# Order of transfer issues in the first chunk, and a weight load cut into ten alternating pieces, in an mLSTM and feed-forward kernel

## The chip, the cores and the metric

The kernel runs on one core of one Trainium2 chip. The time is the device time of one execution in microseconds; it is given as the median of several runs. A core has five engines that run side by side, each through its own list of instructions in order: TensorE (PE, with its weight loads as PEld), VectorE (DVE), ScalarE (ACT), GpSimd (POOL) and SyncE (SP), which here issues nearly all DMA transfers. They meet through semaphores: an instruction that waits holds everything behind it on its engine. The transfers themselves are done by 16 DMA engines. Data that is computed on lies in SBUF (128 partitions), the results of matmuls in PSUM.

## The reference

```python
for t in range(S):                                   # mLSTM, per batch and head, S = 768, D = 40
    m_new  = max(f[t] + m, i[t])
    f_stab, i_stab = exp(f[t] + m - m_new), exp(i[t] - m_new);  m = m_new
    C = f_stab * C + i_stab * outer(v[t], k[t])      # C is 40 x 40
    n = f_stab * n + i_stab * k[t]
    y[t] = sigmoid(o[t]) * (C @ q[t]) / max(abs(n . q[t]), 1)
x = y as (4 * 768) tokens x (8 heads * 40)           # 3072 x 320
h = x @ w_in                                         # 320 x 2048
out = max(0.01 * h, h) @ w_out                       # 2048 x 320
```

There are 4 batches and 8 heads. All arrays are float32 but for the two weight matrices, which come as 8-byte floats: the kernel reads them as 64-bit words and narrows them to float32 itself.

## The kernel before, in words

**Chunks and steps.** The sequence is cut into NB = 6 chunks of 128 positions. A step s is one chunk of one batch: s = 4c + b, steps 0 to 23. The recurrence becomes, per chunk, a 128 x 128 matrix of decays and scores per head, plus a state C carried from chunk to chunk. The feed-forward part of chunk c - 1 is woven into the cell work of chunk c, in units whose order is written out by hand: PE, DVE, ACT and POOL run in the order of the program (`manual_schedule`, L742). SP is not in that list; the framework's scheduler places its transfers.

**The cell part.** `gates(c)` (L237) makes the running sums and maxima of the gates of a chunk for all 32 batch-heads on VectorE, two exponentials on ScalarE, stores the results a and exp(a) to a small DRAM buffer `a_dr` (L254, L260), and for c = 2 and 3 loads the gates of chunk c + 2 (`load_fi`, L262). `u_gates(c)` (L643) transposes its results on PE and copies them to gT and gL on VectorE. `feed(s)` (L665) loads k and v of a step (L302) and spreads a from `a_dr` over the 128 partitions (`spread`, L334). `load_blocks(s, i)` (L312) loads k, q or o_gate of a step in 32-partition blocks, four transfers of 80 KB each (L320). `spread_q` (L336) spreads exp(a) over two halves of 64 partitions (L342). `ahead(s)` (L652) prepares step s: the exponentials of the decays on ScalarE (L376), transposes of k and q on VectorE (L414, L420), then the block loads and `spread_q` of step s + 2, the gated v on GpSimd, and the mask of step s + 1 on GpSimd (`prep_mask`, L368). `u_scores(s)` and `u_mix(s)` are the matmuls of a step; `u_mix` ends by storing x to DRAM (L545), from where `gather_x` (L548) brings it back transposed.

**Buffers.** k/q and v have 4 buffers (step modulo 4), the blocks `rb` and `ea` 2, the decays `w` 4, the gates `fi` 2, the raw weights `raw` 2.

**The weights.** Each matrix is loaded in four quarters: n = 0 to 3 are w_in, n = QN = 4 to 7 are w_out; the text calls them w(0) to w(3), and QN to QN+3. `load_weights(n)` (L171) issues the transfers, `narrow_weights(n)` (L202) is one ScalarE instruction (L213) and six on VectorE (L215 to L229). w_in is laid out in two halves of 64 partitions r = 0, 1, each with five slots of 256 columns; a half takes the five 64-row slices of the matrix in the order `SLOTS[r]`, which is (0, 2, 4, 1, 3) or (1, 3, 0, 2, 4). A quarter of w_in is loaded in four transfers: in each half one that takes three slices with a step of two (384 KB) and one of two slices (256 KB); the first half is issued whole ahead of the second. A quarter of w_out is one transfer of 1280 KB over 128 partitions.

**The first chunk** (`first_chunk`, L669) does steps 0 to 3 with a path of its own: `load` takes k, q and v at once, the scores need PE transposes, `u_x` (L562) brings x to the feed-forward layout by PE and five ScalarE copies. It also narrows w(0) and w(1) and does the first two feed-forward units. Then L744 to L756 issue what chunk 1 needs.

**Chunk 1** (the loop at L764 with c = 1) has 30 units i of the feed-forward part of chunk 0: units 0 to 13 are halves of the first matmul (L588), 14 to 29 are parts of the second (L623), one for each block of tokens and quarter of w_out. `todo` says at which unit a weight quarter is narrowed, `fetch` at which one a quarter of w_out is loaded, `place` after which ones a cell unit follows: scores of step 4 at i = 2, mix of step 4 at 7, scores of 5 at 9, mix of 5 at 11, and so on. After each `u_mix(s)` come the o_gate blocks of s + 2 and `feed(s + 4)`.

Of the kernel before, what the change touches and what calls it, by code (L numbers as in the profile page):

```python
# [18 lines left out]
def kernel(  # L19
# [26 lines left out]
    nc = tc.nc  # L46
    B, H, S, D = q.shape
    P = 128
# [40 lines left out]
    def load_fi(c):  # L89
        t = fi[c] = wk.tile([BH, 2, P], F32, name="fi")  # L90
        eng = nc.scalar if c < 3 else nc.sync
        eng.dma_start(t[:, 0, :], f_all[:, ts(c, P)])
        eng.dma_start(t[:, 1, :], i_all[:, ts(c, P)])
# [69 lines left out]
    def run_of(r, at):  # L163

        ks = SLOTS[r][at:]
        return ks[0], next((i for i in range(1, len(ks)) if ks[i] != ks[i - 1] + 2), len(ks))
# [4 lines left out]
    def load_weights(n):  # L171

        if n < QN:
            dst = w_in[:, n, :]
        else:
            dst = w_out[:, 4 * (n - QN) : 4 * (n - QN + 1), :].rearrange("p a d -> p (a d)")
        to = dst
        if wide:
            if n < 2:
                at = NF * GT - 2 * WC * (n + 1)  # L180
                raw = acts_l[:, at : at + 2 * WC].bitcast(U64)
            elif n == QN:
                raw = w_out[:].rearrange("p f d -> p (f d)")[:, 2 * WC : 4 * WC].bitcast(U64)
            else:
                raw = wk.tile([P, dst.shape[1]], U64, name="raw")[:]
            raws[n] = (raw, dst)
            to = raw
        if n < QN:
            for r in range(2):
                cols = slice(n * QC + 2 * P * r, n * QC + 2 * P * (r + 1))  # L190
                src = moe_w_in[:, cols].rearrange("(k p) c -> p k c", p=DP)
                half = to[DP * r : DP * (r + 1), :].rearrange("p (k c) -> p k c", k=KC)
                at = 0
                while at < KC:
                    k0, n_k = run_of(r, at)
                    nc.sync.dma_start(half[:, at : at + n_k, :], src[:, k0 : k0 + 2 * n_k - 1 : 2, :])
                    at += n_k
        else:
            rows = moe_w_out[(n - QN) * QC : (n - QN + 1) * QC, :]
            nc.sync.dma_start(to.rearrange("p (a d) -> p a d", d=Dm), rows.rearrange("(a p) d -> p a d", p=P))  # L200
# [90 lines left out]
    def load(s):  # L291
        c, b = divmod(s, B)
        rows = ts(c, P)
        d = st[s] = {"kq": kq_t[s % NL], "va": va_t[s % NL]}
        if c == 0:
            parts = [(d["kq"][:, 0, :, :D], k), (d["kq"][:, 1, :, :D], q), (d["va"][:, :, :D], v)]
        else:
            parts = [(d["kq"][:, 0, :, :D], k)] + [
                (d["va"][:, :, QW * n : QW * n + DB], v[:, :, :, DB * n : DB * (n + 1)]) for n in range(2)
            ]  # L300
        for dst, src in parts:
            nc.sync.dma_start(dst, src[b, :, rows, :].rearrange("h p d -> p h d"))  # L302
# [9 lines left out]
    def load_blocks(s, i):  # L312

        c, b = divmod(s, B)
        src = (k, q, o_gate)[i][b, :, ts(c, P), :]
        for r in range(2):
            for n in range(2):
                at = QW - n * (DB if i == 2 else QW)
                rows = slice((2 * r + n) * QW, (2 * r + n + 1) * QW)
                nc.sync.dma_start(  # L320
                    rb_t[s % NR][rows, i, at : at + RL].rearrange("p (j w) -> p j w", j=PR),
                    src[r::2].rearrange("j (p n) d -> p j (n d)", n=TB),
                )
# [12 lines left out]
    def spread_q(s):  # L336

        c, b = divmod(s, B)
        d = st[s]
        d["ea"] = wk.tile([P, PR, P], F32, name="ea", bufs=EAB)  # L340
        for r in range(2):
            nc.sync.dma_start(  # L342
                d["ea"][DP * r : DP * (r + 1)], a_dr[c, 1, b * H + r : (b + 1) * H : 2, :].partition_broadcast(DP),
            )
# [320 lines left out]
    def feed(s):  # L665
        load(s)
        spread(s)

    def first_chunk():  # L669

        for n in range(B):
            load(n)
        load_o(0)
        load_o(1)
        load_weights(0)
        load_o(2)
        load_o(3)
        for n in range(1, 3):
            load_weights(n)
        bu, a = gates(0)  # L680
        warm(14)
        gates_T(0, bu)
        u_transpose(0)
        spread_first(a, 0)
        prep_exp(0)
        prep_vu(0)
        prep_vu(1)
        prepare_tiles()
        u_transpose(1)
        u_scores(0)  # L690
        u_state(0)
        prep_exp(1)
        spread_first(a, 2)
        bus[1] = gates(1)
        u_scores(1)
        u_values(0)
        u_state(1)
        u_transpose(2)
        prep_o(0)
        gate(0)  # L700
        prep_exp(2)
        prep_vu(2)
        w = narrow_weights(0)
        next(w, None)
        u_values(1)
        u_scores(2)
        prep_o(1)
        gate(1)
        u_state(2)
        for _ in w:  # L710
            pass
        u_transpose(3)
        prep_exp(3)
        prep_vu(3)
        prepare_step(0)
        prepare_step(1)
        u_x(0)
        u_values(2)
        u_scores(3)
        u_x(1)  # L720
        u_state(3)
        prep_o(2)
        gate(2)
        w = narrow_weights(1)
        for _ in range(4):
            next(w, None)
        ffs = ff_units(0)
        ffs[0]()
        u_values(3)
        prep_o(3)  # L730
        gate(3)
        u_x(2)
        ffs[1]()
        for _ in w:
            pass
        u_x(3)
        prepare_step(2)
        prepare_step(3)
        return ffs

    E = mybir.EngineType
    with tc.manual_schedule(engines={E.PE, E.DVE, E.Activation, E.Pool}):  # L742
        ffs = first_chunk()
        feed(B)  # L744
        spread_q(B)
        for i in range(3):
            load_blocks(B, i)
        load_weights(3)
        feed(B + 1)
        spread_q(B + 1)  # L750
        for i in range(3):
            load_blocks(B + 1, i)
        load_weights(QN)
        feed(B + 2)
        feed(B + 3)
        load_fi(3)  # L756


        ffs = ffs[2:]
        todo = {0: 2, 3: 3, 8: QN, 12: QN + 1, 17: QN + 2, 22: QN + 3}  # L760
        fetch = {4: QN + 1, 7: QN + 2, 16: QN + 3}
        place = (2, 7, 9, 11, 13, 15, 17, 18, 19)
        now = iter(())
        for c in range(1, NB + 1):  # L764
            if c > 1:
                ffs = ff_units(c - 1)
            cells = cell_units(c) if c < NB else []
            n_ff, n_c = len(ffs), len(cells)
            lead = 2 if c == 1 else 0
            done = fed = 0  # L770
            waiting = []
            for i in range(n_ff):
                if c == 1:
                    if i in todo:
                        for _ in now:
                            pass
                        now = narrow_weights(todo[i])
                    next(now, None)
                    next(now, None)
                    if i in fetch:  # L780
                        load_weights(fetch[i])
                    if i == 0:
                        prep_mask(B)
                        u_gates(1)
                        ahead(B)
                if i == lead and c + 1 < NB:
                    bus[c + 1] = gates(c + 1)
                ffs[i]()
                upto = sum(p <= i for p in place) if c == 1 else min(n_c, (i + 1) * n_c // (n_ff - 8))
                while done < upto:  # L790
                    fn, s = cells[done]
                    fn(s)
                    done += 1
                    if fn is u_scores:
                        ahead(s + 1)
                    elif fn is u_mix:
                        waiting.append(s)
                if i >= n_ff // 2 - 1:
                    for s in waiting:
                        gather_x(s)  # L800
                    waiting.clear()
                while fed < done:
                    fn, s = cells[fed]
                    fed += 1
                    if fn is u_mix:
                        if s + NR < NS:
                            load_blocks(s + NR, 2)
                        if s + NL < NS:
                            feed(s + NL)
# [31 lines left out]
```

## Time and profile before

| | |
|---|---|
| median of 11 runs | 584.75 us (582.55 to 587.31) |
| the profiled execution | 584.8 us, its span 583.0 us |
| mean granted clock of TensorE | 0.941 |
| PE busy | 545.2 us, 94% of the span |
| DVE, ACT, POOL busy | 256.6, 154.5, 110.2 us |
| moved by DMA | 69.89 MB, 120 GB/s in the mean |
| DMA packets | 158412, of these 87072 under 512 B |
| chain that ended last | PE 77%, DVE 10%, DMA 7%, SP's queue 2% |

The profile divides the span into 40 slices and gives each engine's busy share in tenths. Other views list the instructions of an engine in order of time (start, duration, engine, line, operation, and in brackets the idle time before it with what ended it), sum up who waited for whom, follow back the chain of work that ended last, or give sums for chosen windows: the window, its length, then the busy time of PE, PEld, DVE, ACT and POOL with the number of instructions, the granted clock, the share of time that the 16 DMA engines were busy, and the rate in GB/s. "SPq" is SP's own queue: the issuing of a transfer, not the transfer. An issue that takes long stands behind a queue that takes no more.

### The profile page before, as it was taken

How to read it: one execution, taken by the hardware profiler on the slowest of the kernel's cores; microseconds unless marked ns; L12 is line 12 of the kernel's file. 1: busy time of each engine (PE TensorE's matmuls, PEld its weight loads, DVE VectorE, ACT ScalarE, POOL GpSimd, SP SyncE). 2: the span in 40 equal slices, each digit the busy share in tenths (PEclk: the TensorE clock that was granted, in tenths of full speed). 3: DMA queues.
4: the chain of work that ended last, by engine and by line, in shares of the span. 5: the costliest groups of instructions: out<-in, count | busy, mean ns of one | idle time of the engine just before them, and what ended most of it. 6: DMA issues, size and time to landing. Idle time of an engine off the chain costs nothing.

```text
span 583.0 us, 9166 instructions
## 1 busy us (share of the span) xinstructions
PE 545.2 (94%) x3456; PEld 362.6 (62%) x3456; DVE 256.6 (44%) x423; ACT 154.5 (26%) x401; POOL 110.2 (19%) x128
## 2 busy tenths in 40 slices
PE   8988799786569999999999999999999999999997
PEld 7976788554345556765556765566754567744575
DVE  4589779997142643523552704562305552000000
ACT  4465433410004331104341004331023320022100
POOL 4145223153100333110333301331202000000000
PEclk9569779897869999999999999999999999999999
DMA  9998995974851754752665643755533021100000
GB/s 119 168 196 194 176 227 147 271 162 123 214 136 38 162 144 134 176 127 59 156 149 135 160 118 78 164 141 129 162 89 90 26 63 57 45 12 0 1 22 22
DMA packets 158412, 69.89 MB, mean 120 GB/s; under 512 B 87072, under 2 KB 151200, under 8 KB 158368
## 3 DMA queue, kind: packets, MB, share of 16 engines
q1 hardware_dynamic: 157984, 69.18, 50.9%
q8 instruction: 27, 0.44, 0.3%
q10 hardware_dynamic: 384, 0.13, 0.1%
q14 instruction: 17, 0.14, 0.1%
HBM read 61.90 MB, written 7.37 MB: 119 GB/s over the span
## 4 chain that ended last, share of the span: by engine, by line
PE 77%; DVE 10%; DMA 7%; SPq 2%; issue 1%; POOL 1%; ACT 1%; ACTq 0%; DVEq 0%; POOLq 0%
PE ph L588 32%; PE po L623 32%; PE sc L443 3%; PE pT L519 3%; PE pT L525 3%; DMA a_dr<-a 2%; DMA raw<-in_moe_w_out_dram 2%; PE dC L455 2%; DVE kqT L414 1%; DVE kq L420 1%; PE pa L493 1%; DVE w_out L229 1%; DMA va<-in_v_dram 1%; DMA w<-a_dr 1%; DVE w L447 1%
## 5 line engine op out<-in xcount | busy, mean ns | idle before, releaser
L623 PE MATMUL po<-w_out,acts 128*128 128x320 f32 x768 | 221.1, 448 | 20.8 <-DVE w_out L229 17.6
L588 PE MATMUL ph<-xT,w_in 64*128 64x512 f32 (+1 forms) x1120 | 221.3, 546 | 6.4 <-ACT acts L596 6.4
L623 PEld LDWEIGHTS po<-w_out,acts 128*128 128x128 f32 x768 | 148.4, 196 | 86.7 <-DVE w_out L229 18.7
L588 PEld LDWEIGHTS ph<-xT,w_in 64*128 64x128 f32 x1120 | 113.2, 195 | 96.6 <-issue 86.4
L596 ACT ACTIVATE acts<-ph 128x512 f32<-128x512 f32 (+1 forms) x112 | 53.5, 532 | 147.7 <-PE ph L588 147.6
L447 DVE TENSOR_TENSOR w<-w,sc 128x512 f32<-128x512 f32 x48 | 30.8, 681 | 125.2 <-PE sc L443 125.2
L376 ACT ACTIVATE w<-w,gT 128x128 f32<-128x128 f32 x192 | 58.7, 394 | 19.2 <-DVE gL L287 16.2
L628 ACT COPY y<-po 128x320 f32<-128x320 f32 x24 | 10.2, 425 | 195.5 <-PE po L623 185.6
L368 POOL TENSOR_TENSOR w<-w,cmask 128x1024 f32<-128x1024 f32 x20 | 48.0, 2400 | 48.0 <-DMA w<-a_dr 38.2
L466 POOL TENSOR_TENSOR C<-C,gL 64x168 f32<-64x168 f32 x32 | 17.4, 545 | 189.5 <-PE pT L519 188.3
L414 DVE STREAM_TRANSPOSE kqT<-rb 128x512 f32<-128x512 f32 x40 | 41.1, 1103 | 2.7 <-DMA rb<-in_k_dram 2.7
L531 DVE STREAM_TRANSPOSE hb<-pT 128x512 f32<-128x512 f32 x20 | 14.3, 715 | 57.7 <-PE pT L525 57.7
L525 PE MATMUL pT<-w,va 128*64 128x128 f32 x320 | 32.4, 276 | 1.8 <-ACT rb L403 1.5
L538 POOL TENSOR_TENSOR xb<-xb,den 128x320 f32<-128x320 f32 x20 | 14.5, 727 | 100.9 <-DVE xb L535 97.3
L519 PE MATMUL pT<-kq,C 128*64 128x128 f32 x320 | 32.7, 280 | 0.0
L443 PEld LDWEIGHTS sc<-kqT 40*128 40x128 f32 x384 | 27.4, 205 | 8.5 <-issue 8.0
L420 DVE TENSOR_TENSOR kq<-kqT,ea 40x512 f32<-40x512 f32 x40 | 29.0, 725 | 1.4
L443 PE MATMUL sc<-kqT 40*128 40x128 f32 x384 | 29.1, 294 | 0.0
L542 DVE STREAM_TRANSPOSE x<-xb 128x512 f32<-128x512 f32 x20 | 22.2, 1111 | 8.3 <-POOL xb L538 8.3
L525 PEld LDWEIGHTS pT<-w,va 128*64 128x64 f32 x320 | 21.5, 139 | 2.2 <-ACT rb L403 1.7
L519 PEld LDWEIGHTS pT<-kq,C 128*64 128x64 f32 x320 | 20.1, 138 | 2.4 <-issue 2.4
L455 PEld LDWEIGHTS dC<-vu,kq 128*64 128x64 f32 x320 | 12.3, 151 | 13.7 <-issue 10.4
(94 smaller groups left out, 277.9 us busy)
## 6 DMA issues: line engine op xcount, KB each, us to landing
w<-a_dr SPq DMA_DIRECT2D x20, 512.0 KB
rb<-in_k_dram SPq DMA_DIRECT2D x80, 80.0 KB
rb<-in_q_dram SPq DMA_DIRECT2D x80, 80.0 KB
rb<-in_o_gate_dram SPq DMA_DIRECT2D x80, 80.0 KB
ea<-a_dr SPq DMA_DIRECT2D x40, 128.0 KB
kq<-in_k_dram SPq DMA_DIRECT2D x24, 160.0 KB
raw<-in_moe_w_out_dram SPq DMA_DIRECT2D x3, 1280.0 KB
xT<-x_dr SPq DMA_DIRECT2D x40, 96.0 KB
```

The source lines that it names most:

```text
L368: nc.gpsimd.tensor_tensor(w[:], w[:], cmask[:].unsqueeze(1).to_broadcast([P, H, P]), op=ALU.add)
L376: nc.scalar.activation(w[:, h, :], w[:, h, :], AF.Exp, bias=gT[c][:, 0, bh : bh + 1], scale=1.0)
L414: nc.vector.transpose(in_blocks(d["kqT"][:, i]), raw_blocks(s, i, QW).rearrange("p (j n) d -> p j n d", n=TB),)
L420: nc.vector.tensor_tensor(d["qs"][rows], d["kqT"][rows, 1], d["ea"][rows].rearrange("p j t -> p (j t)"), op=ALU.mult,)
L443: nc.tensor.matmul(sc[r][:, j, :], lhsT=kqT[rows, 0, ts(j, P)], rhs=kqT[rows, 1, ts(j, P)], start=True, stop=True,)
L447: nc.vector.tensor_tensor(w[:, r::2, :], w[:, r::2, :], sc[r][:], op=ALU.mult)
L455: nc.tensor.matmul(dC[rows, h // 2].rearrange("p k d -> p (k d)"), lhsT=d["kq"][:, 0, h, :], rhs=d["vu"][:, h].rearrange("p k d -> p (k d) ...
L519: nc.tensor.matmul(pT[DP * r : DP * (r + 1), ts(j, P)], lhsT=C[:, b, j, r, :], rhs=d["qs"][:, ts(j, P)], start=True, stop=False,)
L525: nc.tensor.matmul(pT[DP * r : DP * (r + 1), ts(j, P)], lhsT=d["va"][:, h], rhs=d["w"][:, h, :], start=False, stop=True,)
L588: nc.tensor.matmul(ph[r][:, cols], lhsT=w_row(r, slot, j), rhs=xT[DP * r : DP * (r + 1), slot, cols], start=(slot == 0), stop=(slot == KC ...
L596: nc.scalar.activation(acts[:, f, cols], ph[r][:, cols], AF.Prelu, alpha=0.01)
L623: nc.tensor.matmul(po[n][:], lhsT=acts[:, f, ts(n, P)], rhs=w_out[:, f, :], start=(f == 0), stop=(f == NF - 1),)
```

## The change

1. A quarter of w_in is loaded in ten transfers, one for each slot and half (64 partitions x 256 columns, 128 KB), and the two halves alternate.
2. `load_blocks` issues its four transfers in the order of partitions 0, 64, 32, 96, where it was 0, 32, 64, 96.
3. `u_gates(1)` moves from unit 0 of chunk 1 into the first chunk, between `u_values(1)` and `u_scores(2)`.
4. `gates(2)`, with its two stores and the loads of the gates of chunk 4, moves from unit 2 of chunk 1 into the first chunk, ahead of `u_x(3)`.
5. `feed(6)` and `feed(7)` move from ahead of chunk 1 to its units 2 and 6, so behind the block loads of steps 6 and, for `feed(7)`, of step 7. `load_fi(3)` moves to unit 0, behind `ahead(4)`.
6. The loads of QN+1 and QN+2 move from units 4 and 7 to 5 and 8; QN+2 so comes behind what follows the mix of step 4.

`st.setdefault` only lets `spread_q` come ahead of `load` for a step.

```diff
-            for r in range(2):
-                cols = slice(n * QC + 2 * P * r, n * QC + 2 * P * (r + 1))
-                src = moe_w_in[:, cols].rearrange("(k p) c -> p k c", p=DP)
-                half = to[DP * r : DP * (r + 1), :].rearrange("p (k c) -> p k c", k=KC)
-                at = 0
-                while at < KC:
-                    k0, n_k = run_of(r, at)
-                    nc.sync.dma_start(half[:, at : at + n_k, :], src[:, k0 : k0 + 2 * n_k - 1 : 2, :])
-                    at += n_k
+            src = moe_w_in[:, n * QC : (n + 1) * QC].rearrange("(k p) (r c) -> r p k c", p=DP, r=2)
+            for slot in range(KC):
+                for r in range(2):
+                    nc.sync.dma_start(
+                        to[DP * r : DP * (r + 1), 2 * P * slot : 2 * P * (slot + 1)], src[r, :, SLOTS[r][slot], :],
+                    )
...
-        for r in range(2):
-            for n in range(2):
+        for n in range(2):
+            for r in range(2):
...
         u_values(1)
+        u_gates(1)
         u_scores(2)
...
         for _ in w:
             pass
+        bus[2] = gates(2)
         u_x(3)
...
         load_weights(QN)
-        feed(B + 2)
-        feed(B + 3)
-        load_fi(3)
...
-        fetch = {4: QN + 1, 7: QN + 2, 16: QN + 3}
+        fetch = {5: QN + 1, 8: QN + 2, 16: QN + 3}
...
-            lead = 2 if c == 1 else 0
...
                     if i == 0:
                         prep_mask(B)
-                        u_gates(1)
                         ahead(B)
-                if i == lead and c + 1 < NB:
+                        load_fi(3)
+                    if i in (2, 6):
+                        feed(B + 2 + i // 6)
+                if i == 0 and 1 < c < NB - 1:
                     bus[c + 1] = gates(c + 1)
```

More of the change, by code (lines that the diff above doesn't have):

```diff
@@ L293, in load @@
         rows = ts(c, P)
-        d = st[s] = {"kq": kq_t[s % NL], "va": va_t[s % NL]}
+        d = st.setdefault(s, {})
+        d.update(kq=kq_t[s % NL], va=va_t[s % NL])
         if c == 0:
@@ L338, in spread_q @@
         c, b = divmod(s, B)
-        d = st[s]
+        d = st.setdefault(s, {})
         d["ea"] = wk.tile([P, PR, P], F32, name="ea", bufs=EAB)
```

## The prediction

> **What bounds the kernel now.** I read the page's slices first: from slice 13 on PE is at 9 almost everywhere, and before that it has holes.
>
> ```profile
> PE   8988799786569999999999999999999999999997
>
> DMA  9998995974851754752665643755533021100000
> ```
>
> A slice is 14.6 us, so all the loose time lies ahead of about 175 us; after that the kernel is matmuls back to back and no edit here touches them. Next, who PE waited for (us in all, times, longest), and its timeline around the last hole:
>
> ```profile
> PE po L623 <- DVE w_out L229: 17.6, 3, 12.2
> PE ph L588 <- ACT acts L596: 6.4, 2, 3.4
> PE po L623 <- ACT acts L596: 3.2, 1, 3.2
> ```
>
> ```profile
> 142.12 11.58 PE L623 MATMUL po<-w_out,acts 128*128 128x320 f32 x32 [4.46 <-DVE w_out L229]
> 165.87 11.65 PE L623 MATMUL po<-w_out,acts 128*128 128x320 f32 x32 [12.17 <-DVE w_out L229]
> ```
>
> The longest hole, 12.17 us, ends at 165.87, when the last quarter of w_out has been narrowed. The chain of waits says what that quarter waited for:
>
> ```profile
> 146.84 0.63 SPq L334
> 147.47 0.04 issue
> 147.51 9.77 DMA raw<-in_moe_w_out_dram
> 157.30 1.36 ACT w_out L213
> 158.69 0.84 DVE w_out L215
> ...
> 164.32 1.50 DVE w_out L229
> 165.83 0.04 issue
> 165.87 11.65 PE po L623 x32
> ```
>
> Its raw buffer was free at 120.9 (VectorE's timeline: the second quarter, whose buffer it takes, is narrowed by then), yet SP issued it at 147.51: SP's queue came to it only then. So I asked what SP waited for between 72 and 148. Almost nothing that an engine computes: in 100 to 125 us 5.3 us went to a full DMA queue, in 125 to 148 2.2 us more, and the largest wait for VectorE in either stretch is 0.8. SP runs through a fixed list of transfers, some at its own issue rate and some at the DMA's. **The end is set by how soon SP gets through its list up to that transfer**: PE resumes at 147.51 + 9.77 + 8.59 (ACT and the six VectorE steps) = 165.87.
>
> ```profile
> SPq L320 <- DMA raw<-in_moe_w_out_dram: 5.3, 2, 3.0
> ```
>
> ```profile
> 21.00:24.00 3.00, 3.00 (x27) 2.84 (x27) 2.76 (x10) 0.60 (x2) 0.00 (x0) 0.50 0.98 216
> 32.00:35.00 3.00, 3.00 (x17) 2.96 (x15) 2.92 (x6) 1.93 (x5) 2.43 (x3) 0.51 1.06 214
> 74.00:76.00 2.00, 2.00 (x10) 2.00 (x12) 1.97 (x3) 0.46 (x2) 0.00 (x0) 0.50 1.02 396
> 92.00:98.00 6.00, 6.00 (x82) 5.19 (x82) 5.87 (x8) 2.92 (x10) 0.33 (x1) 1.00 0.52 133
> 102.00:106.00 4.00, 1.22 (x20) 1.00 (x16) 3.62 (x8) 1.25 (x1) 0.69 (x2) 1.00 1.03 410
> ```
>
> In these windows (the last two columns are the DMA's share and GB/s) w_in, loaded by halves of 64 partitions, moves at 214 to 216 GB/s with the DMA full; w_out, over 128 partitions, at 396 and 410. At 92 to 98 the DMA is half idle while SP issues many 80 KB block loads, and at 102 to 106 SP stands behind two quarters of w_out that it issued together at 98.5.
>
> **The change part by part.** The sum is made on SP's list up to 147.51.
>
> *w_in in ten transfers.* Nothing is removed from the bytes: a quarter is 1.31 MB, at 213 GB/s 6.15 us. SP now issues 10 instructions where it issued 4. The 64-partition rows (L196, and L342, L559) cost 0.605 us each, so 10 cost 6.05, which is 3.6 more than before for each of four quarters. What covers it is SP's lead: w(2) was issued by 33.6 and its data ended near 42, and one issue of w(1) stood blocked for 5.06. By issue alone the 30 for quarters 0 to 2 and the o_gate loads between would end at 18.56 + 30 x 0.605 + 1.43 = 38.1, still ahead of 42. For quarter 3 the cover is the second v load behind it, which stands at issue for 5.27 us. Without that cover it costs 3.6. What alternating halves gives is not in the trace as such. The two ends: none, and the 396 GB/s of the 128-partition row (2.8 us a quarter), which SP's issue cuts to 1.55 if an issue costs 0.46 (the 32-partition rows) and to 0.1 at 0.605. Below nothing: at the 0.668 of L334 ten issues cost 6.7, a loss of 0.5 a quarter. The nearest rows speak for little: the windows from 32 to 38 hold several seams between halves and still give 214 and 212; the best half-microsecond (30.5 to 31) gives 258. I take 232 GB/s, 0.5 us a quarter: **-2.0** in all (+2.1 to -6.2).
>
> The Trainium skill, "SBUF — State Buffer", "Can I just issue two DMAs to hit both halves?", speaks against this edit: two transfers to the two halves serialize on the same engines, and gained 6%. The trace agrees with the half rate but has no pair of halves in flight. By that rule, as an estimate, a quarter would gain 0.35 us, this term would be -1.4 and the total 577.4.
>
> *gates(2) in the first chunk.* Its two stores and the two loads of fi(4) leave SP's list between 90.47 and 92.51: -2.04 there. They come back ahead of feed(4). The loads (2 x 0.43) are ready early and land where SP waits anyhow for the store of a(1) to land (33.74 to 43.89, 10.13 in the chain). The stores wait for VectorE's six steps (65.00 to 66.5 now), which move behind the narrowing of w(1), near 54 to 56. **-2.0** (0 to -2.0, and the rival below).
>
> On ScalarE its two exponentials (0.7 us) now stand ahead of the five copies of u_x(3), and wait for VectorE until about 56: the copies end near 57.5 instead of 53.1, and PE's next half starts about 5 us later than 51.80. That falls into PE's 3.07 idle at 59.64 and the 3.36 at 73.72, both waits for ScalarE. VectorE's L215 of w(2) and the transposes after it come 3 to 4 us later, and 1.9 us of gates are then gone from 65. *u_gates(1)* puts three small matmuls (0.7 us at the low clock) ahead of u_scores(2) on PE and 0.4 us of copies on VectorE. None of it reaches the end while VectorE finishes the third quarter no later than some 4 us after its present 142.07: the hole that the sum leaves is 12.2 - 8.0, and VectorE stands idle 16.62 us ahead of 158.69.
>
> *feed(6), feed(7), fi(3), and the fetches.* The transfers stay, the order changes: blocks of step 6 come ahead of feed(6), blocks of 7 and quarter QN+1 ahead of feed(7), and QN+2 goes behind feed(8). So the issue-bound blocks (92 to 98, share 0.52) lie beside transfers that keep the DMA full, and the two w_out quarters no longer block SP together. It can give back the 5.3 us wait at most, and nothing at least; I take **-4.0**. What is late then: w(7), about 10 us later (landing near 97); its mask on GpSimd at 89.21 moves to there and pushes the state scaling at 97.67, whose reader is VectorE's L476 at 105.08. That leaves about 3 us of slack. QN+1 lands near 94, and ScalarE no longer stands 8.26 us for it (PE's 3.21 at 106.43 goes). *load_blocks by halves:* 4 issues take 1.85 us for 320 KB, 173 GB/s, so issue sets it: 0 (with rates up to the 216 of the half, 0.4 a group).
>
> Sum: -2.0 - 2.0 - 4.0 = -8.0. QN+3 is issued near 139.5 and PE resumes near 157.9. The cap is PE's own work: the third quarter's matmuls end at 142.12 + 11.58 = 153.70, so at most 12.2, some 13 with VectorE 1 us earlier. The profiled execution took 584.8 with a span of 583.0; the median is 584.75, so 584.8 - 8.0 = **576.8** stands for both.
>
> **The rivals.** A measurement of this kernel tells about 0.2% (1.2 us) from no change.
>
> *Halves overlap fully* (0.15): the w_in term is -6 instead of -2 and VectorE does not stand in the way: 572.8, down to the cap at 571.5. For it: 396 against 214. Against: the seam windows, and 0.605 an issue.
>
> *Little comes through* (0.17): the halves serialize, the DMA is busy in any order (its share is already 0.92 at 100 to 110), and only 2 to 3 us are left: 582. *Nothing measurable* (0.09): VectorE's later transposes delay SP's buffers as much as SP gains: 584.5.
>
> *SP is held by the stores of a(2)* (0.17), the one that ends slower: SP is in order, and in the program these stores stand ahead of feed(4). If they keep that place, SP reaches them near 35 and waits for VectorE until 56; the spread of step 4 goes out near 58 instead of 43.89. That is +14 on the list, less the 2 and 4: 584.8 + 8 = 593. It decides from a hold of about 8 us, and gives nothing back if the stores come behind 48. Against it: SP's list is not strictly in program order. At 174.13 to 178.54 the store of a(3) is followed by both fi loads and an output, and only then by its second store, which the program has ahead of the loads.
>
> **How the numbers follow.** Forecast 0.42 (576.8); with the rivals faster 0.42 + 0.15 + 0.17 = 0.74, same 0.09, slower 0.17. The range takes in the full overlap, the small gain and no change, up to a slight loss: 571.0 to 586.0; outside stay most of the held queue and the far edge of the overlap, under 2 in 10.
>
> **What would show it.** Right: the last w_out issue near 139 and PE resuming near 158; no 5.3 us block behind a pair of w_out loads; w_in windows at 225 to 250 GB/s; PE idle some 5 us more ahead of u_x(3)'s half and none near 70. Wrong: a w_in window near 400 (overlap), an SP wait for VectorE at the stores of a(2), the mask of step 7 ending after 103, or the last hole set by something other than the last w_out load.

## The result, and the profile after

The changed kernel takes 590.56 us (median of 12 runs, 587.80 to 593.02); the kernel before, in 47 runs beside it, 584.55. The ratio is 1.0102 [1.0085, 1.0119]: **6.0 us slower**, where 576.8 (571.0 to 586.0) was forecast. The profiled execution took 591.45 us, with a span of 589.6 (583.0 before). Lines of code have moved by two to four: L588 is now L586, L623 is L621, L229 is L226, L254 and L260 (the stores to `a_dr`) are L251 and L257, L320 is L318, L334 is L332, L196 is L192.

The slices of the page:

```profile
PE   8974849779659999999999999999999999999997
DMA  9975777976862564651664752754642121100000
```

The last slices are as they were; all that was lost lies ahead of 175 us. The PE row has new dips at its fourth and sixth slice (44 to 59 us and 74 to 88). PE's timeline (start, duration, what, and in brackets the idle time before it) gives them and the two last holes:

```profile
57.24 8.97 PE L586 MATMUL ph<-xT,w_in 64*128 64x256 f32 x60 [7.23 <-ACT xT L572]
...
81.81 8.77 PE L586 MATMUL ph<-xT,w_in 64*128 64x256 f32 x60 [10.38 <-ACT acts L594]
...
154.74 11.86 PE L621 MATMUL po<-w_out,acts 128*128 128x320 f32 x32 [4.76 <-DVE w_out L226]
172.73 11.39 PE L621 MATMUL po<-w_out,acts 128*128 128x320 f32 x32 [6.14 <-DVE w_out L226]
```

The last hole has shrunk from 12.17 to 6.14 us, and yet it ends 6.86 us later: at 172.73, not at 165.87. The third quarter's matmuls before it moved even further, from 142.12 to 154.74. The chain of waits into the last hole is the same chain as before, later:

```profile
153.31 0.67 SPq L332
153.99 0.04 issue
154.03 10.09 DMA raw<-in_moe_w_out_dram
164.12 0.02 issue
164.15 1.37 ACT w_out L210
...
171.18 1.50 DVE w_out L226
172.73 7.36 PE po L621 x17
```

QN+3 is issued at 154.03 where it was issued at 147.51: +6.5 at the issue, +6.9 at PE, +6.6 in the span. So SP's list still sets the end, and the question is where it lost 6.5 us. Its timeline shows the place:

```profile
47.49 1.97 SPq L318 DMA_DIRECT2D rb<-in_k_dram  x4
49.50 1.78 SPq L318 DMA_DIRECT2D rb<-in_q_dram  x3
56.08 0.32 SPq L251 DMA_DIRECT2D a_dr<-a  x1
56.96 0.32 SPq L257 DMA_DIRECT2D a_dr<-bu  x1
57.34 0.41 SPq L318 DMA_DIRECT2D rb<-in_q_dram  x1
57.80 1.84 SPq L318 DMA_DIRECT2D rb<-in_o_gate_dram  x4
59.69 6.29 SPq L192 DMA_DIRECT2D raw<-in_moe_w_in_dram  x10
```

After three of the four q blocks of step 4 SP comes to the two stores of `gates(2)` and issues nothing from 51.28 to 56.08. The fourth q block, the o_gate blocks, the last quarter of w_in and step 5 all stand behind them. SP's waits in 34 to 60 us (us in all, times, longest):

```profile
SPq L251 <- DVE m L265: 4.8, 1, 4.8
SPq L257 <- ACT xT L572: 0.7, 1, 0.7
```

The DMA engines run dry meanwhile. Here is the window from 52 to 57 us, before and then after (the last two columns are the DMA's share and GB/s):

```profile
52.00:57.00 5.00, 4.57 (x40) 3.50 (x38) 4.06 (x6) 2.55 (x6) 3.87 (x6) 1.00 0.77 184
```

```profile
52.00:57.00 5.00, 0.00 (x0) 0.00 (x0) 4.25 (x7) 0.66 (x3) 3.38 (x3) 0.50 0.09 23
```

VectorE came late. `gates(2)` stands behind the narrowing of w(1), which ends at 52.28, and two of its small steps took long:

```profile
50.79 1.49 DVE L226 TENSOR_TENSOR w_in<-w_in,acts 128x1280 f32<-128x1280 f32 x1
52.20 0.40 DVE L241 TENSOR_TENSOR_SCAN F<-fi,zeros 32x128 f32<-32x128 f32 x1
52.53 2.29 DVE L244 TENSOR_SCALAR il<-fi,m 32x128 f32<-32x128 f32 x1
54.85 0.89 DVE L247 TENSOR_TENSOR_SCAN m<-fi,il 32x128 f32<-32x128 f32 x1
55.77 0.28 DVE L249 TENSOR_TENSOR a<-F,m 32x128 f32<-32x128 f32 x1
```

L244 and L247 took 2.29 and 0.89 us; the same two steps took 0.25 and 0.41 at 65.33 and 65.61 in the kernel before (L247, L250 there).

The places that SP passes, in us (start of the issue; each kernel's own profiled execution):

| | spread(4) | w(3) | spread(5) | QN | spread(8) | QN+3 | PE resumes |
|---|---|---|---|---|---|---|---|
| before | 43.89 | 52.50 | 62.14 | 71.47 | 110.59 | 147.51 | 165.87 |
| after | 45.23 | 59.69 | 69.64 | 78.53 | 113.03 | 154.03 | 172.73 |
| gates(2) alone | 44.80 | 59.90 | 69.23 | 79.08 | 116.57 | 153.08 | 171.86 |
| order alone | 43.90 | 52.17 | 61.92 | 71.36 | 105.97 | 146.78 | 164.05 |
| after, stores later | 44.10 | 53.70 | 62.59 | 72.01 | 106.85 | 146.24 | 163.49 |

After minus before reads: +1.34 at spread(4) (no finding: it is issued at 43.7 to 45.9 in the kernels with ten transfers per quarter, at 43.9 to 44.8 in those with four), +5.85 between there and w(3) (the hold), -0.13 to QN, so +7.06 at QN; and from QN to QN+3, where both of the expected gains should lie, only -0.54. One kernel's runs lie some 3 us to either side of their median, so a difference of one or two us between two rows is no finding by itself; the ratios below carry the verdicts. The profiled execution of gates(2) alone lies 1.4 us above its median, those of order alone and of the stores later 1.4 and 2.6 below. From QN to QN+3 the profiled executions that are read here, of kernels that load QN+3 at unit 16, took between 73.2 and 80.5 us; what makes these differ was not followed up.

### The profile page after: what moved, and what is told of

Read it like the earlier page. It is cut to its first block, busy times and chain, and to the rows that moved or that the text cites. A ratio compares the mean times of both kernels' runs of the same rounds, so it can differ in the third digit from the quotient of the medians.

```text
span 589.6 us, 9193 instructions
## 1 busy us (share of the span) xinstructions
PE 541.0 (92%) x3456; PEld 357.2 (61%) x3456; DVE 257.0 (44%) x423; ACT 154.4 (26%) x401; POOL 111.0 (19%) x128
## 4 chain that ended last, share of the span: by engine, by line
PE 74%; DVE 9%; DMA 7%; SPq 6%; issue 2%; ACT 0%; POOL 0%; ACTq 0%; DVEq 0%; POOLq 0%
PE po L621 33%; PE ph L586 31%; PE sc L441 3%; PE pT L523 3%; PE pT L517 3%; SPq L300 3%; DMA raw<-in_moe_w_out_dram 2%; SPq L192 2%; PE dC L453 1%; DMA w<-a_dr 1%; DMA kq<-in_k_dram 1%; DMA ea<-a_dr 1%; DVE kqT L412 1%; SPq L306 1%; DVE w_in L220 1%
## 5 line engine op out<-in xcount | busy, mean ns | idle before, releaser
L586 PE MATMUL ph<-xT,w_in 64*128 64x512 f32 (+1 forms) x1120 | 221.2, 547 | 18.1 <-ACT acts L594 10.4
L621 PE MATMUL po<-w_out,acts 128*128 128x320 f32 x768 | 218.6, 444 | 10.9 <-DVE w_out L226 10.9
L621 PEld LDWEIGHTS po<-w_out,acts 128*128 128x128 f32 x768 | 147.1, 194 | 75.5 <-DVE w_out L226 11.9
L586 PEld LDWEIGHTS ph<-xT,w_in 64*128 64x128 f32 x1120 | 111.9, 196 | 109.7 <-issue 86.5
L523 PE MATMUL pT<-w,va 128*64 128x128 f32 x320 | 36.0, 287 | 8.9 <-DVE w L445 7.8
L517 PE MATMUL pT<-kq,C 128*64 128x128 f32 x320 | 35.4, 288 | 0.0
L523 PEld LDWEIGHTS pT<-w,va 128*64 128x64 f32 x320 | 25.1, 145 | 10.4 <-DVE w L445 8.6
L441 PEld LDWEIGHTS sc<-kqT 40*128 40x128 f32 x384 | 25.7, 195 | 8.5 <-issue 8.0
L418 DVE TENSOR_TENSOR kq<-kqT,ea 40x512 f32<-40x512 f32 x40 | 27.8, 696 | 1.4
L441 PE MATMUL sc<-kqT 40*128 40x128 f32 x384 | 27.5, 284 | 0.0
L517 PEld LDWEIGHTS pT<-kq,C 128*64 128x64 f32 x320 | 23.0, 144 | 2.4 <-issue 2.4
```

The lines of the kernel that those rows point to most:

```text
L418: nc.vector.tensor_tensor(d["qs"][rows], d["kqT"][rows, 1], d["ea"][rows].rearrange("p j t -> p (j t)"), op=ALU.mult,)
L441: nc.tensor.matmul(sc[r][:, j, :], lhsT=kqT[rows, 0, ts(j, P)], rhs=kqT[rows, 1, ts(j, P)], start=True, stop=True,)
L517: nc.tensor.matmul(pT[DP * r : DP * (r + 1), ts(j, P)], lhsT=C[:, b, j, r, :], rhs=d["qs"][:, ts(j, P)], start=True, stop=False,)
L523: nc.tensor.matmul(pT[DP * r : DP * (r + 1), ts(j, P)], lhsT=d["va"][:, h], rhs=d["w"][:, h, :], start=False, stop=True,)
L586: nc.tensor.matmul(ph[r][:, cols], lhsT=w_row(r, slot, j), rhs=xT[DP * r : DP * (r + 1), slot, cols], start=(slot == 0), stop=(slot == KC ...
L621: nc.tensor.matmul(po[n][:], lhsT=acts[:, f, ts(n, P)], rhs=w_out[:, f, :], start=(f == 0), stop=(f == NF - 1),)
```

## The experiments

The theory after the result: SP is held by the stores of a(2), 5 to 6 us, and that is all of the loss; the gains that were to pay for it did not come. Its rivals: the later copies on ScalarE and the later transposes on VectorE cost the time; or the ten transfers do, since SP's issue is now the limit.

**gates(2) back in chunk 1** (all else as after).

```diff
-        bus[2] = gates(2)
         u_x(3)
...
-                if i == 0 and 1 < c < NB - 1:
+                if i == (2 if c == 1 else 0) and c < NB - 1:
```

> The changed kernel with gates(2) back at unit 2 of chunk 1; all else of the change stays. Held queue (SP stands 6 us at the stores of a(2), 50.5 to 57): that hold goes and the two stores and two loads come back into SP's list behind unit 0 (2.0 us): 590.6 - 6.0 + 2.0 = 586.6, with no empty stretch of the DMA near 53 to 56. More issues (the ten transfers per quarter of w_in make it slower): stays at 590. Order (feed(6) and feed(7) behind the block loads make it slower): stays at 590.

Measured: 585.05 us, 1.0012 [0.9982, 1.0043] of the kernel before. The whole loss goes with this one move. The profiled run was 2.6 us above this median, so its trace is not used for sizes. It shows the hold gone, with w(3) at 53.48 and QN at 72.67, but QN+3 only at 153.13: this execution lost the time again between QN and QN+3.

**gates(2) alone**: the kernel before with only that move.

```diff
+        bus[2] = gates(2)
         u_x(3)
...
-                if i == lead and c + 1 < NB:
+                if i == lead and 1 < c < NB - 1:
```

> The kernel before with gates(2) in the first chunk and nothing else of the change. Held queue: the stores stand behind the third block load of q of step 4, SP comes there near 51 and VectorE is done near 56: 5 us of hold, 584.6 + 4.5 = 589. More issues and order: 584.6, as before.

Measured: 588.88 us, 1.0077 [1.0049, 1.0104]. The move alone brings the loss, with the same wait on SP:

```profile
SPq L254 <- DVE bu L256: 5.5, 1, 5.5
```

**The two stores issued by ScalarE**, to free SP and keep the rest as after.

```diff
-            nc.sync.dma_start(a_dr[c, 0], a[:])
+            (nc.scalar if c == 2 else nc.sync).dma_start(a_dr[c, 0], a[:])
...
-            nc.sync.dma_start(a_dr[c, 1], bu[:, 2, :])
+            (nc.scalar if c == 2 else nc.sync).dma_start(a_dr[c, 1], bu[:, 2, :])
```

> The changed kernel, with the two stores of gates(2) issued by ScalarE and not by SP; gates(2) stays in the first chunk. Held queue: SP no longer meets VectorE's wait, the last w_out load goes out 6 us earlier, near 148: 584.6, although VectorE's and ScalarE's part of gates(2) stands where the change put it. If it is the place of gates(2) on VectorE, GpSimd and ScalarE that costs (PE's 7.23 us ahead of u_x(3)'s half), it stays at 590. More issues and order: 590.

Measured: 587.15 us, 1.0056 [1.0036, 1.0076]. Half of the loss stays, so this run did not settle it. Its profiled execution took 584.70 us, 2.45 below the median, so the trace shows where time can go and not how much. SP passes w(3) at 53.78, but that issue stood too:

```profile
53.78 8.77 SPq L192 DMA_DIRECT2D raw<-in_moe_w_in_dram  x10
```

The waits put 2.6 us of it down to the store ("a_dr<-a"), though another engine issued it. Here a rival could still hide: ScalarE's own later work. So the next run left every engine's work where the change put it.

**The stores later**: after, with `gates(2)` computed where the change computes it, and only its two stores issued at unit 2 of chunk 1.

```diff
-        if c > 0:
+        if c > 0 and c != 2:
             nc.sync.dma_start(a_dr[c, 0], a[:])
...
-            nc.sync.dma_start(a_dr[c, 1], bu[:, 2, :])
+            if c != 2:
+                nc.sync.dma_start(a_dr[c, 1], bu[:, 2, :])
...
+                    if i == 2:
+                        nc.sync.dma_start(a_dr[2, 0], bus[2][1][:])
+                        nc.sync.dma_start(a_dr[2, 1], bus[2][0][:, 2, :])
```

> The changed kernel with gates(2) computed in the first chunk as in the change, but its two stores issued at unit 2 of chunk 1. SP then meets no wait, while VectorE, ScalarE and GpSimd run gates(2) where the change put it. Held queue as the whole cause: as e1, 585 (584 to 586.5). If the place of gates(2) ahead of u_x(3) on ScalarE and beside the mask on GpSimd costs by itself: 587 or more.

Measured: 583.96 us, 0.9989 [0.9961, 1.0018]. SP runs through, and the DMA works in the window that was empty:

```profile
49.62 1.85 SPq L319 DMA_DIRECT2D rb<-in_q_dram  x4
51.51 2.13 SPq L319 DMA_DIRECT2D rb<-in_o_gate_dram  x4
53.70 6.28 SPq L192 DMA_DIRECT2D raw<-in_moe_w_in_dram  x10
```

```profile
52.00:57.00 5.00, 0.00 (x0) 0.00 (x0) 4.93 (x5) 0.00 (x0) 4.77 (x6) 0.83 0.69 168
```

PE is as idle in this window as in after (0.00 in its column), since ScalarE's copies for `u_x(3)` are still late. That idle time costs nothing that the medians show. The rival of the later copies and transposes falls; the place of two stores in SP's list is the whole loss, to within this interval (-2.3 to +1.1 us).

**gates(2) sooner**: after, with `gates(2)` ahead of the last three steps of narrowing w(1), so that VectorE is done earlier and the hold gets shorter.

```diff
+        bus[2] = gates(2)
         for _ in w:
             pass
-        bus[2] = gates(2)
         u_x(3)
```

> The changed kernel with gates(2) ahead of the last three narrowing steps of w(1) on VectorE, so 4.2 us sooner (0.8, 1.9 and 1.5 us of steps behind it). Held queue: the stores stand behind the third block load of k of step 4, which SP reaches near 48.9; a(2) is ready near 51, so the hold is 1 to 2.5 us and not 6: 586.5 (585.5 to 587.5). Anything else than the hold in gates(2)'s place: no change, 590.

Measured: 585.75 us, 1.0023 [1.0003, 1.0042]. The stores moved up in SP's list along with `gates(2)`, now behind the third k block, and SP waited 1.0 us in place of 4.8:

```profile
47.93 1.50 SPq L318 DMA_DIRECT2D rb<-in_k_dram  x3
50.31 0.32 SPq L251 DMA_DIRECT2D a_dr<-a  x1
50.69 0.41 SPq L318 DMA_DIRECT2D rb<-in_k_dram  x1
```

```profile
SPq L251 <- DVE bu L253: 1.0, 1, 1.0
```

So the loss follows the length of the hold: 4.8 us with 6.0 lost, 1.0 with 1.3 [0.2, 2.5] (0.0023 of 584.7). The traces order the kernels in the same way. QN is issued at 71.3 to 72.7 us in five kernels without the hold (before, gates(2) back, stores later, and two that follow below, order alone and four alternating; medians 583.96 to 585.05), at 73.45 in this one (585.75), at 75.11 with the stores on ScalarE (587.15), and at 78.53 to 79.16 in the three with the whole hold (after, gates(2) alone, four transfers again; 588.88 to 590.56). That the stores move with VectorE's work suggests that the scheduler puts them where it reckons VectorE to be done, some 5 us too early here; this is inferred from the two placements, not shown.

**The ten transfers alone** (the kernel before with the new w_in loads), and **four transfers again** (after with the old w_in loads). The edits are the first hunk of the change's diff, put in and taken back.

> The kernel before with w_in in ten alternating transfers per quarter and nothing else. Held queue: the issues use up SP's lead, the spread of step 4 comes 1.3 us late as in the changed kernel: 585.9 (584.6 to 586.5). More issues: 24 x 0.63 us are not covered, 589 or more. Halves that overlap fully, as I had allowed: 581 or less.

> The changed kernel with w_in back in four transfers per quarter. Held queue: only SP's lead comes back, the hold stays (it gets longer by what SP is earlier): 589.5, between 588.5 and 590.6. More issues: 585 or less.

Measured: 585.45 us, 1.0022 [0.9995, 1.0049], and 589.95 us, 1.0083 [1.0055, 1.0111]. Ten transfers gain nothing either way; SP was held all the same in the second (6.4 us at L254).

**Four transfers that alternate between the halves**: the kernel before with its own pieces in the order half 0, half 1, half 0, half 1.

```diff
-            for r in range(2):
...
-                at = 0
-                while at < KC:
+            at = [0, 0]
+            while min(at) < KC:
+                for r in range(2):
...
+                    at[r] += n_k
```

> The kernel before with the four transfers of a quarter of w_in in alternating order of the halves (384, 256, 256, 384 KB), so that SP's issue, 2.4 us a quarter, cannot be the limit. Halves that serialize: the rate from 32 to 40 stays at 214 to 220 GB/s and the time at 584.6. Halves that run together: a rate well over 230 there, and up to 2 us less.

Measured: 584.16 us, 0.9991 [0.9966, 1.0017]: no change in time. But the window from 30 to 40 us, with w(1) and w(2) in it, tells apart what two halves can do and what ten issues do. Before, after, and this kernel:

```profile
30.00:40.00 10.00, 8.21 (x70) 7.20 (x66) 8.98 (x11) 6.61 (x20) 5.84 (x9) 0.67 1.05 214
```

```profile
30.00:40.00 10.00, 6.40 (x61) 5.74 (x61) 9.00 (x10) 8.86 (x24) 5.84 (x9) 0.84 0.79 207
```

```profile
30.00:40.00 10.00, 7.26 (x44) 6.08 (x43) 8.80 (x10) 7.70 (x23) 5.84 (x9) 0.50 1.05 226
```

Alternating alone gives 226 GB/s for 214, +6%; in the window that was named ahead of the run, 32 to 40 us, it gives 232 for 215, +8%. So it falls between what was expected of halves that serialize and of halves that run together. The Trainium skill ("SBUF — State Buffer", "Can I just issue two DMAs to hit both halves?") states that two concurrent transfers, one to each half, measured 6% over a single one. This trace comes near that. In ten pieces the rate is 207 and the DMA's share falls from 1.05 to 0.79: the DMA waits for SP, whose ten issues take 6.29 us, 0.63 each. The other traces agree: from 32 to 40 us the kernels with ten pieces have 203 to 210 GB/s at a share of 0.74 to 0.81, those with four in the old order 211 to 215 at 1.04 to 1.06.

**The order alone**: the kernel before with the change's points 5 and 6.

```diff
-        feed(B + 2)
-        feed(B + 3)
-        load_fi(3)
...
-        fetch = {4: QN + 1, 7: QN + 2, 16: QN + 3}
+        fetch = {5: QN + 1, 8: QN + 2, 16: QN + 3}
...
+                        load_fi(3)
+                    if i in (2, 6):
+                        feed(B + 2 + i // 6)
```

> The kernel before with feed(6), feed(7), load_fi(3) and the loads of QN+1 and QN+2 in their new places, nothing else. My prediction: 4 us less, 580.6. Held queue, with the reading that SP's stand behind a quarter of w_out only moves to the next load of many small packets: no gain, 584.6 (583.5 to 586). Order as the cause of the loss: 588 or more, with GpSimd's mask of step 6 near 91 and VectorE's wait for the state scaling of step 4.

Measured: 584.46 us, 0.9994 [0.9974, 1.0014]. The 4 us of the forecast are not there. SP reaches spread(8) 4.6 us earlier, as the forecast had it, and loses it at once. This is SP behind a quarter of w_out, before:

```profile
101.66 6.76 SPq L320 DMA_DIRECT2D rb<-in_o_gate_dram  x4
```

and with the new order:

```profile
106.73 0.43 SPq L200 DMA_DIRECT2D raw<-in_moe_w_out_dram  x1
107.26 2.51 SPq L321 DMA_DIRECT2D rb<-in_k_dram  x4
109.87 6.81 SPq L321 DMA_DIRECT2D rb<-in_q_dram  x4
```

```profile
SPq L321 <- DMA raw<-in_moe_w_out_dram: 4.5, 1, 4.5
...
SPq L321 <- DMA w_out<-in_moe_w_out_dram: 2.4, 1, 2.4
```

Before, 5.3 us of such waits came behind the pair of quarters, QN+1 and QN+2; now 4.5 come behind QN+2 by itself, and the 2.4 behind QN, where step 6's blocks now follow it (71.36). Block loads issued behind one quarter stand nearly as long as behind two. The kernel before shows this already, behind QN+3 alone, in 148 to 170 us:

```profile
SPq L320 <- DMA raw<-in_moe_w_out_dram: 4.5, 1, 4.5
```

QN+3 is issued 0.7 us earlier.

**The last quarter earlier**: if SP's list sets the end by the place of one transfer, moving that transfer alone should gain. The kernel before, with QN+3 loaded at unit 13 and not at 16.

```diff
-        fetch = {4: QN + 1, 7: QN + 2, 16: QN + 3}
+        fetch = {4: QN + 1, 7: QN + 2, 13: QN + 3}
```

> The kernel before with the last quarter of w_out fetched at unit 13 and not 16; nothing else. If SP's list sets the end, its issue comes at about 125 and not 147.5, lands long before VectorE gets to it, and PE's hole of 12.2 goes: 573.5 (572.5 to 577). If something else ends at the same time (gather of x, blocks of the next steps, each 3.4 us later), the gain is under 5: 580 or more.

Measured: **577.76 us, 0.9869 [0.9843, 0.9894]**, the lowest median of all, and clearly below both kernels. QN+3 is issued at 126.81, and the last two quarters of w_out run as one:

```profile
109.06 6.47 PE L623 MATMUL po<-w_out,acts 128*128 128x320 f32 x16 [5.75 <-ACT acts L596]
...
143.59 19.19 PE L623 MATMUL po<-w_out,acts 128*128 128x320 f32 x64 [5.81 <-DVE w_out L229]
165.78 7.33 PE L588 MATMUL ph<-xT,w_in 64*128 64x512 f32 x20 [3.00 <-DMA xT<-x_dr]
174.93 3.17 PE L588 MATMUL ph<-xT,w_in 64*128 64x512 f32 x12 [1.82 <-ACT y L628]
```

The 12.17 us hole is gone. The 64 matmuls end at 162.78, where before they ended at 177.52: 14.7 us earlier. Of these PE then gives back 8.2. It waits 3.00 for x's transposed load and 1.82 at 174.93, and loses 3.4 in the 32 matmuls of the last two lines: they take 7.33 and 3.17 us, where the same 32 took 7.07 from 177.52 on in the kernel before. The granted clock was 0.77 in 165.78 to 173.11, and 1.00 in 177.52 to 184.59 before. So the span ends 6.5 us shorter (576.5), and 573.5 was not reached: the expectation took the hole as gained whole.

**Both, on the new order**: the order alone, and after with the stores later, each with QN+3 at unit 13 (`fetch = {5: QN + 1, 8: QN + 2, 13: QN + 3}`).

> The kernel before with the new places of feed(6), feed(7), load_fi(3), QN+1 and QN+2, and the last quarter of w_out fetched at unit 13. In the kernel with the last quarter early, PE still stood 5.8 us at 109 for ScalarE, which stood behind QN+1's landing; with the new places QN+1 goes out some 6 us earlier, so that stand goes: 577.8 - 3 = 575 (573 to 578). If the order is worth nothing here either: 577.8.

> The changed kernel with the stores of gates(2) issued at unit 2 and the last quarter of w_out fetched at unit 13. Held queue: with the hold gone and the list's last weight early, both ends are off: 575 (573 to 578). If gates(2) in the first chunk or the ten transfers cost by themselves, it stays behind the kernel with the order and the early quarter alone by 2 or more.

Measured: 578.80 us, 0.9899 [0.9867, 0.9930], and 578.25 us, 0.9894 [0.9866, 0.9922]. Both lie just above the range that was expected, 573 to 578. Neither is better than the one moved transfer on the kernel before (its interval overlaps theirs), so the rest of the change adds nothing there either.

## Why the prediction was wrong

- **What bounds the kernel: right.** "The end is set by how soon SP gets through its list up to that transfer" held in both directions: +6.5 us at the issue of QN+3 gave +6.9 at PE and +6.6 in the span, and taking it 20.7 us earlier gave 0.9869, up to where VectorE's narrowing of the third quarter sets PE's start (143.59).
- **gates(2): the step that failed.** It was put at -2.0; alone it measures +4.5 (588.88 less the 584.33 of its comparison), since SP stands 5.5 us at the first of its stores. The step reckoned what the two stores free at 90.47 and left what they hold at their new place to a rival with a chance of 0.17. That rival had the right mechanism, and was wrong in two ways. Its place: the stores went neither to 35 nor where VectorE is done, but to 51.3, so the hold was 4.8 + 0.7, not 21. And its break-even: "a hold of about 8 us", nothing given back "if the stores come behind 48". The stores came behind 48 and still cost all of the result, because the 8 us were the forecast's own credits, and those of the order and of w_in were not there. The credit of 2.0 for gates(2) itself may be: from QN to QN+3 the trace of gates(2) alone takes 74.00 us, the kernel before 76.04, which is no more than single executions differ by.
- **That VectorE is done near 54 to 56** was nearly right (56.3), and that PE's next half starts about 5 us later too (57.24 for 51.80). Both lie beside other work: with the stores later they cost nothing.
- **The order: mis-sized.** Put at -4.0 (0 to -5.3), measured -0.3 us [-1.5, +0.8] (0.9994 of 585.0). The 5.3 us stand was read as the fault of a pair of w_out quarters issued together. It is that of block loads behind any one quarter, and moved along: 4.5 us behind QN+2, 2.4 behind QN; the 4.5 us behind QN+3 in the kernel before had the answer.
- **w_in in ten transfers: mis-sized, and not by the halves.** Put at -2.0 (+2.1 to -6.2), measured +1.3 [-0.3, +2.9] alone, so not told from nothing. Alternating halves do load at about the 232 GB/s that were taken (226 and 232 in the two windows). But 10 issues at 0.63 us are as long as the data (6.3 against 6.15 us), so the DMA waits for SP. And the step took a faster load for a shorter list: the four alternating transfers have the rate, yet spread(4) goes out at 43.96 for 43.89 and the time stays (0.9991). The cover by SP's lead held, nearly: the sum put the end of the first 30 issues at 38.1, it was 40.49.
- **The hole counted one for one.** The sum takes every us off the last hole as a us off the time. When QN+3 was fetched early the whole hole of 12.17 us went, and the time fell by 7.2 (584.99 to 577.76), less than the 8.0 that were forecast for a part of it.
- **A condition that failed beside it.** The forecast needed VectorE to finish the third quarter within 4 us of 142.07. It let PE start it at 154.74 in after, and at 148.11 with the stores later:

```profile
148.11 11.93 PE L622 MATMUL po<-w_out,acts 128*128 128x320 f32 x32 [3.29 <-DVE w_out L226]
163.49 10.57 PE L622 MATMUL po<-w_out,acts 128*128 128x320 f32 x32 [3.45 <-DVE w_out L226]
```

The third quarter's matmuls there end at 160.04; had the 8 us come, PE could still not have resumed at 157.9. QN+2 is fetched later with the new order (113.77 in after, 107.56 with the stores later, at most 99.6 before), and PE's third quarter starts later in the same two kernels. With the order alone QN+2 goes out at 106.73, some 7 us later than before, and PE starts the third quarter at 144.17, only 2 us later, so the late fetch by itself does not explain the rest; what does stays open. What the rows show is that a late third quarter shortens the last hole from its front.

- **Two readings were off and carry nothing.** 320 KB in 1.85 us are 177 GB/s and not 173 (a KB of the profile is 1024 bytes), and the six steps of the gates end 1.5 us after they start (65.00 to 66.5), not 1.9.

What stays open: the 2.6 us that SP stood on a store that ScalarE had issued; the scheduler's rule for placing stores, inferred only; the new place of `u_gates(1)` and the new order in `load_blocks`, never run by themselves (with all else but the stores' place they come to 0.9989).

## What to carry to other kernels

A store that waits for another engine, in a queue that runs in order, holds every load behind it: price it by when its producer is really done and what stands behind it, not by the slot that it leaves. Where one transfer's place in a queue sets the end, move that transfer; making the queue around it shorter moves the waits along, and here one changed number gave 1.3% where a rewritten order gave nothing. Before a load is cut into more pieces, compare the pieces' issue time with the time of the data.

## What the runs showed of the hardware that was not expected

- A load over 64 partitions costs SP 0.63 us to issue whether it moves 128 KB or three times that (0.605 and up in the kernel before), so at 128 KB the issue, not the DMA, sets the rate: 207 GB/s at a DMA share of 0.79.
- A small VectorE step took 2.29 us and not 0.25 while GpSimd ran its mask over the same time:

```profile
52.27 2.46 POOL L366 TENSOR_TENSOR w<-w,cmask 128x1024 f32<-128x1024 f32 x1
```

The step starts at 52.53 and ends at 54.82, the mask at 54.73. The same stands in the traces of five more kernels in which `gates(2)` runs at this place (gates(2) alone, the stores on ScalarE, four transfers again, and the two with the stores later): 2.29 us each time, with the end 0.08 to 0.09 us behind the mask's. Where `gates(2)` runs elsewhere the step took 0.25 us, and 0.89 in gates(2) sooner, where it overlaps a shorter GpSimd instruction (48.53 to 49.25). No run took the mask away and left the step in place. The 2.0 us by which the step was longer are a part of the 4.8 that SP waited.
